# ScalarE's routing one-hots spread over the P·V groups by a table, and the third batch's placing steps moved ahead of its choice of expert

## The chip, the cores and the metric

One core of one Trainium2 chip. The metric is the device time of one execution in microseconds, the median of several; lower is better.

## The reference, cut to what matters

Three layers, one after another. Attention with queries pooled in twos (4 batches, 8 heads, 1152 keys, 576 pooled queries, width 64):

```python
q_pool = q.reshape(B, H, S // 2, 2, D).mean(axis=3)
attn = softmax(q_pool @ k.T / sqrt(D));  x = attn @ v      # x: 2304 tokens of 512
```

Then a mixture of 8 experts in which each token goes to one expert, and a soft mixture behind it:

```python
logits = x @ w_gate + modality_bias[modality_id]
e_idx = np.argmax(logits, axis=1)                          # the routing
out[mask] = gate_w[mask, None] * (np.maximum(x[mask] @ w1[e], 0) @ w2[e])
```

The change is in how the routing of the tokens is worked out while attention is still running. No arithmetic of it changes.

## The kernel before, in words

Attention goes over 16 **pairs** of heads, `p` = 0 to 15, four to a batch: batch 0 is pairs 0 to 3, and so on. A pair has 36 **positions** (`pos`): 2 halves of the queries, 9 blocks of 128 keys, 2 heads. Each position is two matmuls on TensorE, `S1` (L252) and `S2` (L258), into one of three PSUM banks named `sc`, and one exp on ScalarE (`e<-sc`, L262). So an exp that comes late holds up the `S1` three positions on. `maxpiece` (L203, L205) is a matmul into one of three banks `mx` and a maximum on VectorE; it looks for the row maxima of the next pair, and `maxrow` (L223, L226) writes them into `QL`, without which the next pair can't start.

Every sixth position (2, 8, 14, 20, 26, 32) ends with a **group**: the P·V matmuls of three key blocks (`pv`, L272), during which TensorE makes no scores and ScalarE has room, and three additions `acc` on GpSimd (L283, L285), which sum the exps for the softmax. An `e` tile (9 buffers) comes free when its P·V and its addition are done. Besides the exps, ScalarE has in fixed places: at 2 and 8 the casts of a later pair (`KC` twice, `QC`, L158 and L168), at 14 and 26 the copy `sgS` (L310), at 2 and 20 the copy `xu` (L275).

All engines take their instructions in the order in which the program was written; there is no planner. The routing of a batch is written as a list of small steps, `queue`, put together by `in_order` at position 18 (`RT`) of pairs 4, 8 and 12, and at certain positions one step is taken from it:

- `choose`: six VectorE steps that find each token's expert; `gates`: an exp on ScalarE, four VectorE steps (L415 to L418) and the DMA that stores the tokens (`xs`); `rest`: steps that do nothing.
- `place`: `ranks` (TensorE, L357 to L361), five small VectorE steps that end with the conversion `rdf` (L398), then **one-hots**: 24 activations on ScalarE (`far`, L373, and `rA` or `rR`, L374, alternating, two for each of 12 matrices), then `table` (TensorE, L367), which multiplies them.
- `count`: two VectorE steps (L410, L411) that keep the running counts per expert.

One-hots are not taken one by one: at each of the six group positions up to `NHOT` = 4 of them are issued ahead of the group. For batch 0 the four choosing steps and the gates fall in pair 4, ranks and placing in pair 5, one-hots at 26 and 32 of pair 5 and at 2, 8, 14 and 20 of pair 6, the table at 22 of pair 6, the counts behind it; batch 1 likewise in pairs 8 to 10.

For batch 2 (pairs 12 to 14) there is a further list: `expert` (L976 to L991) picks the expert with the most rows, so that its weights can be fetched early by two GpSimd DMAs (`ahead.fetch(0)`, `fetch(1)`, L744), and `rows` comes behind the table. There the order before is ranks, counts, three rests, expert, the two fetches, the five placing steps, one-hots, table. The one-hots fall in pair 14, whose group positions also hold a cast on ScalarE (`split`, L765, 128x512) and a subtraction on VectorE (L766) of the fetched weights.

Of the kernel before, what the change touches and what calls it, by code (L numbers as in the profile page):

```python
# [17 lines left out]
HP = H // 2  # L18
# [19 lines left out]
HPOS = 4  # L38
NI = N // 128
NB = E * (N // TS)  # L40
NHOT = 4
XW = DM + 8
QSTEP = 2
GS = 3
LAG = 3
# [11 lines left out]
MR = (29, 32)  # L57
# [4 lines left out]
RT = 18  # L62
# [24 lines left out]
def attention(ctx, tc, g):  # L87
# [27 lines left out]
    ahead = g["ahead"] = Ahead(tc, g, KS, KH, QS, QL, KX, QX, KC, KL, QLc, QC, VT)  # L115
    pairs = [(b, hp) for b in range(B) for hp in range(HP)]
    n = len(pairs)
# [18 lines left out]
    def load_v(p):  # L136
        b, hp = pairs[p]
        nc.sync.dma_start(out=st[p]["v"], in_=vT[b, hp])
# [51 lines left out]
    def maxpiece(p, m):  # L190
        s = st[p]
        j, blk, t = pieces[m]
        ks = slice(t * 384, (t + 1) * 384)
        mps = ps.tile([128, 512], F32, name="mps", tag="mx", bufs=3)
        if j is None:
            if p == 0:
                for j in range(2):
                    nc.tensor.matmul(mps[:, :384], s["QB"][:, j], s["KS"][:, j, ks], start=(j == 0), stop=(j == 1))
            else:
                nc.tensor.matmul(mps[:, :384], QB, KC[:, ks], start=True, stop=True)  # L200
            slot = 8
        else:
            nc.tensor.matmul(mps[:, :384], s["QS"][:, j, blk * 128:(blk + 1) * 128], s["KS"][:, j, ks], start=True, stop=True)  # L203
            slot = 4 * j + blk
        V.reduce_max(s["mxp"][:, slot, t:t + 1], mps[:, :384], axis=AX.X)  # L205
# [81 lines left out]
    def group(p, g_):  # L287
        steps = range(GS * g_, GS * g_ + GS)
        for step in steps:
            PV(p, step)  # L290
        for step in steps:
            if (p, step) != (n - 1, 2 * NKB - 1):
                accadd(p, step)
# [129 lines left out]
    def in_order(r, select=None):  # L423
        choose, place, count, gates = r

        rest = [lambda: None] * 3
        if select is None:
            return choose[:4] + rest[:2] + gates + choose[4:] + rest[:1] + place + count
        expert, rows = select
        place = place[:1] + count + rest + expert + [lambda i=i: ahead.fetch(i) for i in range(2)] + place[1:]  # L430
        return choose[:3] + rest + gates + choose[3:] + rest + place + rows[:1] + rest + rows[1:]

    def first():

# [100 lines left out]
    nc.sync.dma_start(out=wgbd[0:64, :, 0:E], in_=wg[0])  # L535
    nc.sync.dma_start(out=wgbd[64:128, :, E:2 * E], in_=wg[1])
    consts = g["route_consts"]()
    queue = []
    for p in range(n + 1):
        work = {}  # L540

        def at(pos, *fs):
            work[pos] = work.get(pos, []) + list(fs)

        mp = lambda q, m: (lambda: maxpiece(q, m))
        NP = len(pieces)
        if p == 0:
            for i, m in enumerate(range(NP0, NP)):
                at(P0[0] + i * P0[1] // 8, mp(0, m))
            at(P0[0] + P0[1] + 1, lambda: maxred(0, [3, 4]))  # L550
            at(P0[0] + P0[1] + 2, lambda: maxrow0(0, [(288, 384), (384, 512), (512, 576)]))
            for i, m in enumerate([24, 25, 26] + list(range(24))):
                at(P1[0] + i * P1[1] // NP, mp(1, m))
            for i in range(3):
                at(33 + i, mp(2, 24 + i))
        elif p + 1 < n:
            for pos, m in zip(MA1, range(24)) if p == 1 else zip(MA, range(3, 24)):
                at(pos, mp(p + 1, m))
            if p + 2 < n:
                for pos, m in zip(MB, (24, 25, 26, 0, 1, 2)):  # L560
                    at(pos, mp(p + 2, m))
        if p + 2 < n:
            for pos, f in zip(PREP0 if p == 0 else PREP, prep(p + 2, nc.gpsimd if p == 0 or p >= HP and p % HP < 2 else None)):
                at(pos, f)
        if p < n:
            if p + 1 < n:
                late = 3 if p == 0 else 0
                at(MR[0] + late, lambda: maxred(p + 1, [0, 1, 2, 3, 4]))
                at(MR[1] + late, lambda: maxrow(p + 1))
            late = 4 if p in (0, n - 1) else 2 if p >= HP and p % HP == 0 else 0  # L570
            at(FA[0] + late, lambda: fin0(p, 0))
            at(FA[1] + late, lambda: fin1(p, 0))
            if pairs[p][1]:
                at(FA[2], lambda: fin2(p, 0))
        if p > 0:
            if pairs[p - 1][1] == 0:
                at(FC, lambda: fin2(p - 1, 0))
            fb = FE if p < 4 else FB if p < n - HP else FZ
            at(fb[0], lambda: fin0(p - 1, 1))
            at(fb[1], lambda: fin1(p - 1, 1))  # L580
            if p < n:
                at(fb[2], lambda: fin2(p - 1, 1))
                if pairs[p - 1][1] == HP - 1:
                    at(RT, lambda: queue.extend(in_order(route(pairs[p - 1][0]), ahead.select() if p == n - HP else None)))
        if p == n - 2:
            for i in range(2, 6):
                at(AF2[i - 2], lambda i=i: ahead.fetch(i))
            for i in range(6):
                at(6 * i + 2, lambda i=i: ahead.split(i))
        if p == n - 1:  # L590
            at(0, lambda: ahead.fetch(6), lambda: ahead.fetch(7))
            at(14, lambda: ahead.load_x(0), lambda: ahead.load_x(1))
            at(26, lambda: ahead.turn(0))
            at(28, lambda: ahead.turn(1))
            at(29, ahead.gates)
            for i in range(6):
                at(6 * i + 2, lambda i=i: ahead.split(6 + i))
        if p == n:
            group(n - 1, 2 * NKB // GS - 1)
            assert not queue  # L600
            mm, ev = ahead.mm, ahead.ev

            def both(*fs):
                return [f[i] for i in range(max(map(len, fs))) for f in fs if i < len(f)]

            mm(0)
            ev(0)
            fin0(n - 1, 1)
            mm(1)
            fin1(n - 1, 1)  # L610
            ev(1)
            choose, place, count, gates = route(B - 1)
            ta, tb = g["make_tasks"](ps, count)
            rest = gates[1:]
            run = lambda fs: [f() for f in fs]
            run(choose[:3])
            mm(2)
            run(both(choose[3:], gates[:1]))
            fin2(n - 1, 1)
            ev(2)  # L620
            mm(3)
            place[0]()
            ta[0]()
            ev(3)
            mm(4)
            mm(5)
            table = place.pop()
            chain = both(place[1:], ta[1:], rest)
            for i, f in enumerate(chain):
                f()  # L630
                if i in TAIL:
                    u = 4 + TAIL.index(i)
                    ev(u)
                    if u < 6:
                        mm(u + 2)
            mm(8)
            mm(9)
            table()
            mm(10)
            tb[0]()  # L640
            cut = lambda u: (lambda: ahead.split(u))
            g["rest"] = [cut(12), cut(13), lambda: mm(11), cut(14), cut(15)] + [lambda u=u: mm(u) for u in range(12, 16)] + [lambda: ev(15)]
            break

        units = [(u, c, j) for u in range(2) for c in range(NKB) for j in range(2)]
        for z in units[:3]:
            S1(p, *z)
        for pos, z in enumerate(units):
            if pos >= 3:
                S1(p, *z)  # L650
            S2(p, *z)
            for f in work.get(pos, []):
                f()
            if p and pos % CST == 0 and consts:
                consts.pop(0)()
            if queue and pos >= (8 if p < n - 3 else 0) and (pos % 3 < 2 if p % HP == 0 or p > n - HP else pos % QSTEP == 0) and callable(queue[0]):
                queue.pop(0)()
            if pos % (2 * GS) == LAG - 1:
                for _ in range(NHOT):
                    if queue and not callable(queue[0]):  # L660
                        queue.pop(0)[1]()
            if pos == LAG - 1 and p > 0:
                group(p - 1, 2 * NKB // GS - 1)
            elif pos >= 2 * GS and pos % (2 * GS) == LAG - 1:
                group(p, pos // (2 * GS) - 1)
            if pos == 3 and p + 3 < n:
                if p == 0:
                    load_v(2)
                load(p + 3)
# [1071 lines left out]
```

## Time and profile before

| what | value |
|---|---|
| median of 3 runs | 814.7 us (814.34 to 814.75) |
| the profiled execution | 816.65 us, of which the span from first to last instruction is 814.9 us |
| TensorE busy | 782.9 us, 96% of the span |
| VectorE / ScalarE / GpSimd busy | 565.8 / 461.2 / 541.8 us |
| granted TensorE clock | 0.996 |

Busy shares are means over the whole program. Whether an engine with time to spare still holds up TensorE is read from a stretch of it, here from one pair of heads and from single positions in it.

### The profile page before, as it was taken

The page shows a single profiled execution, that of the slowest core. Times are in us where ns is not written, and L with a number is a line of the kernel's source. Part 1 is how long each engine was busy: PE and PEld are TensorE (multiplying, and loading weights), DVE is VectorE, ACT ScalarE, POOL GpSimd, SP SyncE. Part 2 cuts the span into 40 slices and gives each one's busy share as a digit, 9 for nine tenths or more (in the row PEclk, how much of TensorE's full clock was granted, in tenths as well). Part 3 has the DMA queues.
Part 4 walks back from the last instruction along what each step waited for, and adds up shares of the span by engine and source line. Part 5 has one row for each costly group of instructions (what it writes and reads, how often), then busy time and mean ns, then how long its engine had stood idle before and what let it go on. Part 6 is the DMA issues. An engine that isn't in the chain of part 4 may idle for free.

```text
span 814.9 us, 15864 instructions
## 1 busy us (share of the span) xinstructions
PE 782.9 (96%) x5674; PEld 595.9 (73%) x5674; DVE 565.8 (69%) x1171; ACT 461.2 (57%) x1096; POOL 541.8 (66%) x501
## 2 busy tenths in 40 slices
PE   5899999999999999999999999999999999999897
PEld 5677777766677776777666668788898689988356
DVE  7587777678777877877878785766666556664252
ACT  5456565666865658766556873455555545554133
POOL 6879899999888988879978963534635544450200
PEclk9999999999999999999999999999999999999999
DMA  9876558667655676755554120786787887767987
GB/s 323 232 208 157 156 146 221 158 172 178 148 158 149 149 199 168 176 136 151 127 141 140 52 80 12 223 291 237 274 279 264 261 287 260 272 208 260 341 364 233
DMA packets 57782, 162.80 MB, mean 200 GB/s; under 512 B 14443, under 2 KB 21915, under 8 KB 53595
## 3 DMA queue, kind: packets, MB, share of 16 engines
q1 hardware_dynamic: 41604, 98.05, 42.7%
q0 software_dynamic: 13648, 47.32, 17.4%
q10 hardware_dynamic: 2448, 16.39, 5.6%
q8 instruction: 46, 0.75, 0.4%
q14 instruction: 36, 0.29, 0.1%
HBM read 110.45 MB, written 10.89 MB: 149 GB/s over the span
## 4 chain that ended last, share of the span: by engine, by line
PE 82%; DVE 5%; ACT 4%; POOL 3%; issue 3%; DMA 2%; SPq 0%; ACTq 0%; POOLq 0%; DVEq 0%
PE pv L272 17%; PE sc L252 12%; PE sc L258 8%; PE mps L203 7%; PE hp L774 4%; PE hp L776 4%; PE hp L775 4%; PE yp L788 4%; PE yp L790 3%; PE yp L789 3%; PE sg L305 2%; PE hp L1472 2%; PE op L1486 2%; PE tp L332 2%; DVE mxp L205 1%
## 5 line engine op out<-in xcount | busy, mean ns | idle before, releaser
L285 POOL TENSOR_TENSOR acc<-acc,e 128x576 f32<-128x576 f32 x214 | 315.2, 1473 | 23.6 <-ACT e L262 10.1
L262 ACT ACTIVATE e<-sc 128x288 f32<-128x288 f32 x576 | 223.7, 410 | 138.8 <-PE sc L258 116.1
L205 DVE TENSOR_REDUCE mxp<-mps 128x1 f32<-128x384 f32 x432 | 220.5, 549 | 94.2 <-PE mps L203 86.4
L252 PE MATMUL sc<-QS,KS 128*128 128x288 f32 x576 | 186.0, 331 | 3.3 <-ACT e L262 3.1
L258 PE MATMUL sc<-QL,KH 69*128 69x288 f32 x576 | 170.0, 298 | 1.5 <-DVE QL L223 1.2
L272 PE MATMUL pv<-e,V 128*64 128x288 f32 x1152 | 161.8, 416 | 0.0
L252 PEld LDWEIGHTS sc<-QS,KS 128*128 128x128 f32 x576 | 109.2, 190 | 56.4 <-issue 27.1
L203 PE MATMUL mps<-KS,QS 128*128 128x384 f32 x384 | 134.9, 356 | 11.5 <-ACT QS L468 7.0
L744 POOL DMA_INDIRECT wraw<-in_w,widx x72 | 73.9, 1026 | 106.3 <-DVE wlo L766 82.7
L272 PEld LDWEIGHTS pv<-e,V 128*64 128x64 f32 x1152 | 74.4, 137 | 60.2 <-issue 22.2
L258 PEld LDWEIGHTS sc<-QL,KH 69*128 69x128 f32 x576 | 109.3, 190 | 2.0 <-DVE QL L223 1.4
L766 DVE TENSOR_TENSOR wlo<-wraw,whi 128x512 fp32r<-128x512 f32 x136 | 90.7, 689 | 27.1 <-ACT whi L765 22.8
L765 ACT CAST whi<-wraw 128x512 fp32r<-128x512 f32 x136 | 79.6, 619 | 18.2 <-DMA wraw<-in_w,widx 14.0
L203 PEld LDWEIGHTS mps<-KS,QS 128*128 128x128 f32 x384 | 74.4, 194 | 14.8 <-ACT QS L468 7.4
L774 PE MATMUL hp<-xh,whi 128*128 128x256 f32 x256 | 73.2, 286 | 0.0
L776 PE MATMUL hp<-xh,wlo 128*128 128x256 f32 x256 | 71.9, 281 | 1.0 <-issue 0.8
L775 PE MATMUL hp<-xl,whi 128*128 128x256 f32 x256 | 71.8, 280 | 0.3 <-DVE xl L761 0.3
L283 POOL TENSOR_TENSOR acc<-e 128x576 f32<-128x576 f32 x31 | 44.7, 1441 | 35.8 <-ACT e L262 35.7
L781 ACT ACTIVATE hh<-hp 128x256 fp32r<-128x256 f32 x64 | 24.5, 384 | 72.8 <-PE hp L776 55.6
L782 DVE SCALAR_TENSOR_TENSOR hl<-hp,hh 128x256 fp32r<-128x256 f32 x64 | 27.1, 424 | 42.7 <-ACT hh L781 39.6
L788 PE MATMUL yp<-whi,hh 128*128 128x512 f32 x128 | 53.0, 414 | 0.7 <-ACT hh L781 0.6
L774 PEld LDWEIGHTS hp<-xh,whi 128*128 128x128 f32 x256 | 48.1, 188 | 4.8 <-ACT whi L765 1.3
(397 smaller groups left out, 1233.2 us busy)
## 6 DMA issues: line engine op xcount, KB each, us to landing
mw<-in_m2w SPq DMA_DIRECT2D x17, 1024.0 KB, 6.8
mw<-in_m2w ACTq DMA_DIRECT2D x15, 1024.0 KB, 7.2
V<-in_vT SPq DMA_DIRECT2D x16, 576.0 KB, 3.6
KX<-in_kT SPq DMA_DIRECT2D x15, 576.0 KB, 4.0
QX<-in_qT SPq DMA_DIRECT2D x15, 576.0 KB, 5.9
KS<-KC SPq DMA_DIRECT2D x30, 288.0 KB, 5.3
KH<-KC SPq DMA_DIRECT2D x30, 288.0 KB, 4.6
QS<-QC SPq DMA_DIRECT2D x60, 144.0 KB, 3.9
```

The source lines that it names most:

```text
L203: nc.tensor.matmul(mps[:, :384], s["QS"][:, j, blk * 128:(blk + 1) * 128], s["KS"][:, j, ks], start=True, stop=True)
L205: V.reduce_max(s["mxp"][:, slot, t:t + 1], mps[:, :384], axis=AX.X)
L252: nc.tensor.matmul(sc[:, :NU], s["KS"][:, j, c * 128:(c + 1) * 128], s["QS"][:, j, u * NU:(u + 1) * NU], start=True, stop=False)
L258: nc.tensor.matmul(sc[:, :NU], s["KH"][0:69, j, c * 128:(c + 1) * 128], s["QL"][0:69, j, u * NU:(u + 1) * NU], start=False, stop=True)
L262: nc.scalar.activation(s["e", u, c][:, j], sc[:, :NU], AF.Exp, scale=SM)
L272: nc.tensor.matmul(pv[j * 64:(j + 1) * 64, :NU], s["v"][:, j, c, :], e[:, j], start=(c == 0), stop=(c == NKB - 1))
L285: eng.tensor_add(s["acc", u], s["acc", u], s["e", u, c])
L766: nc.vector.tensor_sub(lo, x, hi.bitcast(F32))
L774: nc.tensor.matmul(hp, wh[:, c], xh[:, k], start=(k == 0), stop=False)
L775: nc.tensor.matmul(hp, wh[:, c], xl[:, k], start=False, stop=False)
L776: nc.tensor.matmul(hp, wl[:, c], xh[:, k], start=False, stop=(k == DM // 128 - 1))
L788: nc.tensor.matmul(yp[h], hh[:, hs], wh, start=(f == 0), stop=False)
```

## The change

- `NHOT` becomes a table by position (2, 0, 2, 2, 2, 4 at 2, 8, 14, 20, 26, 32), and `NHOT2` (3, 3, 3, 3, 3, 4) for pair 14. So 24 one-hots spread over more groups: for batch 0 from 26 of pair 5 to 20 of pair 7, for batch 2 from 26 of pair 13 to 32 of pair 14.
- The one-hots get a list of their own, `hots`, which is drawn on once the step `ready` has run; the queue goes on meanwhile, so `count` now runs in pair 5 (at 28 and 30). When the list is empty, what must follow (`after`: the table, for batch 2 also `rows`) is put in the queue.
- In pairs 4 and 8 one step is taken at every position below 29, where before it was at two positions of three up to the end; one rest less stands ahead of the gates.
- Batch 2: the placing steps stand among the expert steps, ahead of the fetches. Taken one by one, the expert steps stood at 18, 19, 21, 22, 24, 25 of pair 13 and the fetches at 27 and 28; now they stand at 18, 21, 25, 27, 28, 30 and at 31 and 33. Placing, which stood at 30 to 34 and at 0 of pair 14, is at 13, 15, 16, 19 and 22.

```diff
-NHOT = 4
+NHOT = {2: 2, 8: 0, 14: 2, 20: 2, 26: 2, 32: 4}
+NHOT2 = {2: 3, 8: 3, 14: 3, 20: 3, 26: 3, 32: 4}
...
+        hots.extend(f[1] for f in place if not callable(f))
+        table = [place.pop()]
+        place = [f for f in place if callable(f)]
+        ready = lambda: hot.append(True)
         if select is None:
-            return choose[:4] + rest[:2] + gates + choose[4:] + rest[:1] + place + count
+            return choose[:4] + rest[:1] + gates + choose[4:] + rest[:1] + place + [ready] + count, table
         expert, rows = select
-        place = place[:1] + count + rest + expert + [lambda i=i: ahead.fetch(i) for i in range(2)] + place[1:]
-        return choose[:3] + rest + gates + choose[3:] + rest + place + rows[:1] + rest + rows[1:]
+        place = (place[:1] + count + place[1:4] + expert[:1] + place[4:5] + expert[1:2] + place[5:] + [ready] + expert[2:]
+                 + [lambda i=i: ahead.fetch(i) for i in range(2)])
+        return choose[:3] + rest + gates + choose[3:] + rest + place, table + rows[:1] + rest + rows[1:]
...
-            if queue and pos >= (8 if p < n - 3 else 0) and (pos % 3 < 2 if p % HP == 0 or p > n - HP else pos % QSTEP == 0) and callable(queue[0]):
+            if queue and pos >= (8 if p < n - 3 else 0) and (pos % 3 < 2 if p >= n - HP else pos < MR[0] if p % HP == 0 else pos % QSTEP == 0):
                 queue.pop(0)()
-            if pos % (2 * GS) == LAG - 1:
-                for _ in range(NHOT):
-                    if queue and not callable(queue[0]):
-                        queue.pop(0)[1]()
+            if pos % (2 * GS) == LAG - 1 and hot:
+                for f in hots[:(NHOT2 if p == n - 2 else NHOT)[pos]]:
+                    hots.pop(0)()
+                if not hots:
+                    hot.clear()
+                    queue.extend(after)
+                    after.clear()
```

## Rows read from the trace of the kernel before

**Rows 1.** Exps in stretches of one pair: stretch, length, busy (count), clock, DMA, GB/s

```profile
170.60:201.65 31.05, 14.05 (x36) 1.00 0.87 221
201.65:232.20 30.55, 13.78 (x36) 1.00 0.56 147
232.20:260.60 28.40, 14.20 (x36) 1.00 0.60 159
...
288.95:318.87 29.92, 13.95 (x36) 1.00 0.90 229
...
406.25:438.45 32.20, 14.21 (x36) 1.00 0.59 155
438.45:469.30 30.85, 13.02 (x36) 1.00 0.22 69
```

**Rows 2.** ScalarE in order of time, position 8 of pair 6

```profile
207.39 0.66 ACT L158 CAST KC<-KX 128x576 fp32r<-128x576 f32 x1
...
208.53 0.36 ACT L373 ACTIVATE far<-i,rdf 96x72 f32<-96x72 f32 x1
...
209.27 0.49 ACT L373 ACTIVATE far<-i,rdf 96x256 f32<-96x256 f32 x1
...
210.21 2.37 ACT L262 ACTIVATE e<-sc 128x288 f32<-128x288 f32 x6
```

**Rows 3.** ScalarE in order of time, position 8 of pair 7 (in brackets: idle before)

```profile
239.16 2.51 ACT L262 ACTIVATE e<-sc 128x288 f32<-128x288 f32 x6 [0.47 <-PE sc L258]
```

**Rows 4.** TensorE in order of time, ranks in pair 5

```profile
181.21 0.26 PE L357 MATMUL rp<-oh,trir 96*96 96x48 f32 x1
...
182.10 0.46 PE L272 MATMUL pv<-e,V 128*64 128x288 f32 x2
```

**Rows 5.** TensorE in order of time, table in pair 6

```profile
220.33 0.87 PE L367 MATMUL tbp<-rR,rA 96*72 96x256 f32 x6
221.04 0.29 PE L252 MATMUL sc<-QS,KS 128*128 128x288 f32 x1
```

**Rows 6.** VectorE in order of time, second half of pair 4

```profile
163.18 0.56 DVE L205 TENSOR_REDUCE mxp<-mps 128x1 f32<-128x384 f32 x1 [1.16 <-PE mps L203]
...
166.32 1.04 DVE L416 TENSOR_SCALAR sm<-sm 96x6 f32<-96x6 f32 x1
...
170.07 0.75 DVE L418 COPY xr<-sm 96x48 f32<-96x48 f32 x1
```

**Rows 7.** TensorE in order of time, first positions of pair 5

```profile
171.34 0.45 PE L203 MATMUL mps<-KS,QS 128*128 128x384 f32 x1 [0.48 <-DVE mxp L205]
```

**Rows 8.** ScalarE in order of time, position 2 of pair 14

```profile
439.50 0.61 ACT L765 CAST KS<-KX 128x512 fp32r<-128x512 f32 x1
440.62 0.35 ACT L373 ACTIVATE far<-i,rdf 96x72 f32<-96x72 f32 x1 [0.50 <-DVE rdf L398]
```

**Rows 9.** VectorE in order of time, expert steps of batch 2 in pair 13

```profile
426.90 1.28 DVE L988 TENSOR_SCALAR aone<-akey,amx 128x8 f32<-128x8 f32 x1
...
430.59 0.15 DVE L991 SCALAR_TENSOR_TENSOR awidx<-aex,pioq 128x4 int32<-128x4 f32 x1
```

**Rows 10.** GpSimd in order of time, around the first fetches

```profile
428.24 1.41 POOL L285 TENSOR_TENSOR acc<-acc,e 128x576 f32<-128x576 f32 x1
431.05 1.24 POOL L744 DMA_INDIRECT KX<-in_w,awidx  x1 [1.40 <-DVE awidx L991]
...
438.14 0.97 POOL L744 DMA_INDIRECT KX<-in_w,awidx  x1
439.12 5.29 POOL L285 TENSOR_TENSOR acc<-acc,e 128x576 f32<-128x576 f32 x3
```

**Rows 11.** GpSimd in order of time, last additions of pair 14

```profile
471.24 4.75 POOL L285 TENSOR_TENSOR acc<-acc,e 128x576 f32<-128x576 f32 x3
```

**Rows 12.** ScalarE in order of time, positions 15 and 16 of pair 15

```profile
479.44 0.74 ACT L262 ACTIVATE e<-sc 128x288 f32<-128x288 f32 x2 [1.10 <-PE sc L258]
```

**Rows 13.** A stretch behind the third fetch: all engines' busy time, clock, DMA share, GB/s

```profile
439.70:441.90 2.20, 2.20 (x19) 1.57 (x15) 2.20 (x4) 1.63 (x5) 2.12 (x2) 1.00 0.81 238
```

More of the change, by code (lines that the diff above doesn't have):

```diff
@@ L537, in attention, with begin @@
     consts = g["route_consts"]()
-    queue = []
+    queue, hots, hot, after = [], [], [], []
+    def begin(now, later):
+        queue.extend(now)
+        after.extend(later)
     for p in range(n + 1):
@@ L583, in attention @@
                 if pairs[p - 1][1] == HP - 1:
-                    at(RT, lambda: queue.extend(in_order(route(pairs[p - 1][0]), ahead.select() if p == n - HP else None)))
+                    at(RT, lambda: begin(*in_order(route(pairs[p - 1][0]), ahead.select() if p == n - HP else None)))
         if p == n - 2:
@@ L599, in attention @@
             group(n - 1, 2 * NKB // GS - 1)
-            assert not queue
+            assert not queue and not hots and not after
             mm, ev = ahead.mm, ahead.ev
```

## The prediction

> **What bounds the kernel now.** I read the profile's first page, then the exps of ScalarE pair by pair, then single positions in the order of time, then the list of waits. TensorE is busy 96% of the span at full clock, so only time that TensorE loses can be won. Since the engines take their work in program order, the pairs of attention are copies of one another, and a longer pair shows what disturbed it. An undisturbed pair takes 28.40 us (pair 7; pairs 4, 8 and 12 are within 0.1 of it). The pairs with routing behind them take 31.05, 30.55 and 29.92 (pairs 5, 6 and 9; pair 10 repeats pair 6), and batch 2's take 32.20 and 30.85 (pairs 13 and 14) [rows 1]. The excess is 4.80 for batch 0, some 3.65 for batch 1 (1.52 and the repeated 2.15) and 6.25 for batch 2: 14.7 us in all. The question is how much of it the new places free.
>
> The reader is to see how the one-hots lengthen a pair. At position 8 of pair 6 ScalarE runs two casts from 207.39 and four one-hots from 208.53, with no idle time, and the next exp starts only at 210.21 [rows 2]. At the same place of pair 7, without one-hots, ScalarE has 0.47 us left over before its next exp [rows 3]. So the four take 1.68 where 0.47 is free. The delay of the exp is 1.2 or so, of which TensorE, with two more score banks in hand, gets back a few tenths. The one-hots come in twos: 0.74 us for the pair on 72 columns (208.53 to 209.27) and 0.94 on 256 (209.27 to 210.21) [rows 2].
>
> **What must stay.** Ranks hold TensorE from 181.21 to 182.10, 0.89 us [rows 4], and the table from 220.33 to 221.04, 0.71 us [rows 5]. Both are only moved (the table from pair 6 to pair 7). A pair that opens a batch also ends with fewer transposes and passes them on to the next one; I put 0.3 on that, an estimate, about a third of the 0.89 that the eight matmuls of ranks take. That is 1.9 us per batch that no placing can remove.
>
> **Batches 0 and 1.** The excess of batch 0 less 1.9 is 2.9; that of batch 1 is 1.75.
>
> - The one-hots at 2 and 8 of pair 6 are 2.15 less the table's 0.71, so 1.45 us of it, in batch 1 the same. Position 8 gets none now. Position 2 gets one pair of 0.94 instead of 1.68, in front of the `xu` copy that waits for P·V anyway. I take both as gone. The groups at 14, 20 and 26 get 0.74 to 0.94; less than half of what they hid or nearly hid before. Position 32 keeps four, which before cost nothing there. Bounds: all of it gone, or 0.3 left at two positions of each batch.
> - What is left, 1.45 in batch 0 and 0.3 in batch 1, is the late start of pair 5 and the first one-hots at 26, where four waited for `rdf` and two will now. The start: at the end of pair 4 VectorE is late, as the gates' L416 (1.04) and L418 (0.75) fall among the row maxima [rows 6], and TensorE waits for a maximum 0.48 us before it can load position 1's piece [rows 7]. One step per position brings these gates to 25 to 27, and there VectorE sat idle for 1.16 us [rows 6]. I take that stall as gone. If the front-loaded steps are late there, 0.5 comes back in each of pairs 4 and 8.
> - Cost: `count` moves into the end of pair 5 (and 9) ahead of `maxrow`. Its addition is of the kind of L416, 1.04 us [rows 6], or nothing if VectorE has that idle time; from the stall of 0.48 [rows 7] at the upper end to 0, I take 0.15 per batch. Late next would be `QL` for the next pair.
>
> Sum: 2.9 - 0.15 = 2.75 and 1.75 - 0.15 = 1.6, together 4.35 us, between 3.0 and 4.65.
>
> **Batch 2, pair 14.** Before, the first four one-hots waited 0.50 us for `rdf` behind the cast [rows 8], then took their 1.68. With `rdf` in pair 13, and three in place of four at five of the six groups, 0.4 us leaves each of them. Pair 14's excess is 2.45, of it the table 0.71; of the other 1.7 I take 1.4 as gone. ScalarE's room at such a group is about 1.6 to 2.0: the 2.82 from the first cast to the exp at position 8 of pair 6 less the 1.2 by which it was too much, and the few tenths that the banks hide [rows 2]. The cast's 0.61 and three one-hots (1.3) are 1.9, just inside it. Bounds 0.8 and 1.7.
>
> **Batch 2, pair 13.** The placing steps that came at its end now stand among the expert steps; `ranks`, the store of `xs` and the counts stay where they were. In the trace L988 takes 1.28 and L991 0.15, both on 128x4 or 128x8 [rows 9]; L416, on 96x6, took 1.04 [rows 6]. So a small VectorE step costs 0.15 to 1.3 us here, and five moved ones add 0.75 to 6.5 to the stretch from 13 to 22, with L395 to L398 likely about half that. They delay row maxima and may hold TensorE; L988 and L989, which sat before `sgS` at 26, move past it. I take these to cancel but for a gain of 0.5, bounds -1.0 and +0.8.
>
> **Batch 2, GpSimd.** This is what I looked for a new wait in. `fetch(0)` waited for `awidx`, written at 430.59, and began at 431.05 [rows 9, 10]. The step that writes it goes from position 25 to 30. Those five positions hold the group at 26: at 28.40 us for 36 positions five are 4 us, and VectorE's lag may shrink or grow, so I take `awidx` at 435.0, bounds 434.0 and 437. GpSimd works in program order, and the three additions of the group at 32 stand behind `fetch(0)`, `fetch(1)` behind them. From 435.0: 1.24 for the fetch [rows 10], three additions of 1.41 to 1.48 [rows 10], then two fetches of 0.97, which ends near 442.7 where the trace had the next additions begin at 439.12 [rows 10]. That is 3.6 late, or about 3.4, since these additions took 5.29 rather than 4.4 [rows 10], some of which will not recur. GpSimd has little idle time after it, so pair 14's last addition, which ended at 475.99 (471.24 + 4.75) [rows 11], ends near 479.4. The exp at position 16 of pair 15 needs the buffer that this frees. It began at about 479.8, as the second from 479.44 [rows 12], so 3.8 us of slack. With 3.4 of it gone and TensorE 1.9 earlier, ScalarE would wait 1.5 us. TensorE hides part of it with its score banks, and I take 0.75 as lost, bounds 0 and 2.5.
>
> The weights themselves: a tile of 0.5 MB that was issued at 438.14 [rows 10] has its bytes moved by 441.9 (238 GB/s for 2.20 us is that tile) [rows 13], 3.8 us. From 435.0 it lands at 438.8; the first cast began at 439.50 with no idle time before it [rows 8] and will come 0.5 earlier. It is just in time. If `awidx` is at its upper bound, ScalarE stands 2 us at position 2.
>
> Sum for batch 2: 1.4 + 0.5 - 0.75 = 1.15, between -2.5 and 2.5.
>
> In all 4.35 + 1.15 = 5.5 us. The profiled execution took 816.65 with a span of 814.9, so I expect a span near 809.4 and 811.15 with what lies around it; that execution is 1.95 above the median of the runs, and on the median of 814.7 the forecast is 809.2. A saving in attention should reach the end whole, since what follows waits for the routing of the last batch.
>
> **The rivals.**
>
> - *GpSimd takes all of batch 2's gain, and more.* If `awidx` comes at 437, the late additions and the late weights together cost about 2.5 more than I took. For it: the slack of 3.8 [rows 12] is nearly used. Against: it needs VectorE to lag 2 us more than I take, on top of the 4.4 by which `awidx` moves. Total gain 2.0 to 2.5 (2.0 for the additions, about 1 for the cast at position 2), time near 812.5.
> - *The moved steps are blocked, and the time gets worse.* Suppose that each of the five moved steps takes 1.3 as L988 did [rows 9]. Then `awidx` is 6.5 us later still, at 441, the additions are 9.9 late against 3.8 of slack [rows 12], and from a lag of about 9 us on batch 2 loses more than the 4.35 won elsewhere: about 9.9 - 3.8 = 6.1 lost, time 816.4. Against it: L991 among the same neighbours took 0.15, so not every step is hit. Of the trace's two kinds of duration the Trainium skill gives a reason (SBUF — State Buffer, Who interferes with whom): VectorE and GpSimd share a port pair that one instruction holds from start to end, and a VectorE step with two SBUF inputs or in a two-port mode is shut out for as long as the GpSimd one lasts. By that rule a moved step costs up to one addition (1.41), the five up to 7 us, and the time would be 817; the 1.28 of L988 agrees, the 0.15 of L991 is a case in which nothing was in the way.
> - *The bursts were not what cost.* If the excess of pairs 6 and 10 were TensorE's own work, spreading would move and not free it; only the stall at the start of pair 5 and the wait for `rdf` go, 1 to 1.5 us, time 813.5. Against it: ScalarE is gapless at position 8 of pair 6 and idle in pair 7 [rows 2, 3].
>
> **How the numbers follow.** The forecast with its bounds (gain 3.5 to 7) has 0.65, a gain above 7 has 0.05, GpSimd taking batch 2's gain 0.16, bursts not the cause 0.07, worse 0.07. The measurement of this kernel can tell 0.2%, 1.6 us, from no change. Of the third rival about half lies within 1.6, and a little of the first: faster 0.86, same 0.07, slower 0.07. The range: below, a gain of 7.0, nearly all upper bounds together (4.65 + 2.5), 807.7, and I go to 807.4; above, the first rival at 812.5 and a little beyond, 812.8. That leaves out the third rival, the worse one, and the few best cases.
>
> **What would show it.** Pair 6 and pair 10 near 28.4, pairs 7 and 11 near 29.1 (the table), pairs 5 and 9 near 29.7, pair 14 near 29.4 and pair 13 near 31.7. ScalarE idle again before the exp behind position 8 of pair 6. At the start of pair 5 no wait of TensorE for a maximum. `awidx` near 435 and the last additions of pair 14 some 2 to 3 us nearer to the exp that needs them, with waits of exps on GpSimd in pair 15. The forecast is wrong if pairs 7 and 11 grow by more than the table, if pair 5 keeps its late start or pair 9 gets one from the counts, or if pair 15 stretches by more than 1 us.

## The result and the profile after

The change makes the kernel slower: 821.03 us against 814.73 (medians of 6 runs each), ratio 1.007 with a 95% interval of 1.0042 to 1.0097 (ratios here compare all executions, so they can differ from the quotient of two medians). The forecast was 809.2, range 807.4 to 812.8. The six executions spread from 817.56 to 823.78 and the mean granted clock goes along, from 0.994 in the fastest to 0.987 in the slowest; the kernel before stayed within 814.2 to 816.4. The profiled execution is the fastest of them (817.56, span 815.8), so its rows show the least of the loss.

Pair by pair, as in [rows 1], with pairs 8 and 10 besides:

```profile
169.10:199.65 30.55, 14.09 (x36) 1.00 0.63 175
199.65:228.05 28.40, 14.20 (x36) 1.00 0.61 158
228.05:257.15 29.10, 14.22 (x36) 1.00 0.60 155
257.15:287.05 29.90, 14.23 (x36) 1.00 0.62 152
287.05:317.30 30.25, 14.26 (x36) 1.00 0.66 186
317.30:345.75 28.45, 14.20 (x36) 1.00 0.60 158
...
403.25:436.90 33.65, 14.20 (x36) 1.00 0.51 132
436.90:471.95 35.05, 13.71 (x36) 0.90 0.23 75
```

Pairs 6 and 10 are down from 30.55 to 28.4, an undisturbed pair, and pair 7 is up by the table's 0.7: the one-hots are hidden, as forecast. Pair 5 went from 31.05 to 30.55 only, pair 9 from 29.92 up to 30.25, and pair 8, undisturbed before, to 29.90. From pair 4 to 12 the sum fell by 1.7 us (264.15 to 262.45). Then batch 2 gives it back and more: pair 13 from 32.20 to 33.65, pair 14 from 30.85 to 35.05, with a mean clock of 0.90 in it.

The spans of the two profiles differ by only 0.9, since two stretches outside these pairs were shorter after the change. Pair 4 starts at 140.80 instead of 142.10: the profile before has its clock at half for a while in pair 0, which the change does not touch, and the profile after does not. TensorE's busy time there, with the clock behind the count:

```profile
33.90:37.30 3.40, 3.40 (x16) 0.50 1.00 376
```

Behind pair 14 it is another 1.75, which was not followed up.

**Pair 14.** TensorE in the order of time around position 26, the idle time before an instruction in brackets, and GpSimd's last additions before it:

```profile
456.01 0.29 PE L259 MATMUL sc<-QL,KH 69*128 69x288 f32 x1
459.78 0.69 PE L306 MATMUL sg<-acc,ones 128*32 128x288 f32 x2 [3.48 <-POOL acc L286]
```

```profile
456.86 2.87 POOL L286 TENSOR_TENSOR acc<-acc,e 128x576 f32<-128x576 f32 x2
```

`sg` sums the exps of the first half of the queries from `acc`. The addition that it needs ends at 459.73, and TensorE, which takes its work in order, stands still for 3.48 us. In the kernel before the same addition ended at 458.41 and `sg` began at 459.27, 0.86 us to spare. Counted from the start of pair 14 the addition is 2.87 later than before (22.83 instead of 19.96) and TensorE is there 1.42 earlier (19.40 instead of 20.82): these two, less the 0.86 to spare, make 3.43 of the 3.48. So 1.4 of the wait is time that TensorE had won by the new places of batch 2's steps and one-hots.

```profile
456.66 1.75 POOL L285 TENSOR_TENSOR acc<-acc,e 128x576 f32<-128x576 f32 x1
```

```profile
459.27 0.44 PE L305 MATMUL sg<-acc,ones 128*32 128x288 f32 x2
```

Why GpSimd is late is in its own order of time, which answers to [rows 10]:

```profile
427.28 1.41 POOL L286 TENSOR_TENSOR acc<-acc,e 128x576 f32<-128x576 f32 x1
432.87 1.24 POOL L758 DMA_INDIRECT KX<-in_w,awidx  x1 [4.18 <-ACT e L263]
434.15 4.43 POOL L286 TENSOR_TENSOR acc<-acc,e 128x576 f32<-128x576 f32 x3
438.73 1.31 POOL L758 DMA_INDIRECT QX<-in_w,awidx  x1 [0.15 <-issue]
```

GpSimd sits idle for 4.18 us ahead of the fetch, where it was 1.40. The index `awidx` is written at 432.41, and the additions of the group at 32, the first of which had its exps by then, stand behind the fetch in program order. (The bracket names an exp; the fetch itself reads only the index.)

During the stall the clock falls. Busy time of all engines by stretch, with the granted clock behind the counts:

```profile
450.00:458.00 8.00, 6.19 (x43) 4.78 (x42) 5.42 (x13) 5.49 (x15) 7.61 (x6) 1.00 0.01 2
458.00:464.80 6.80, 5.02 (x21) 2.27 (x22) 2.11 (x1) 2.08 (x5) 6.18 (x6) 0.50 0.39 128
464.80:472.00 7.20, 7.04 (x50) 5.42 (x48) 5.40 (x13) 5.17 (x14) 6.51 (x6) 1.00 0.09 27
```

6.8 us at 1.2 GHz, of which the first 1.8 belong to the stall itself.

**Pair 13.** Two of the moved placing steps on VectorE, and the transposes on TensorE that wait behind them:

```profile
418.49 0.90 DVE L396 CAST rdi<-dest 96x6 int32<-96x6 f32 x1
419.31 0.54 DVE L206 TENSOR_REDUCE mxp<-mps 128x1 f32<-128x384 f32 x1
419.77 1.10 DVE L397 TENSOR_SCALAR rdi<-rdi 96x6 int32<-96x6 int32 x1
```

```profile
420.00 0.38 PE L318 MATMUL sgT<-ident,sgS 80*96 80x80 f32 x3 [0.93 <-DVE mxp L206]
...
421.39 0.53 PE L333 MATMUL tp<-ident,xu 128*96 128x128 f32 x3 [0.53 <-DVE mxp L206]
```

The steps work on 96x6 numbers and take 0.90 and 1.10. They stand between row maxima; these free the PSUM banks that `sgT` and `tp` share with them. The two waits make 1.46 us. In the kernel before, TensorE waited in pair 13 elsewhere, in front of `sg`, and this wait is gone:

```profile
428.79 0.44 PE L305 MATMUL sg<-acc,ones 128*32 128x288 f32 x2 [0.53 <-DVE mxp L205]
```

So the growth of 1.45 is a net figure: some 2.0 paid, of which 0.5 shows in no single wait, and 0.53 won. Experiment 7 separates the two.

**Pair 8.** The same kind of thing in the front-loaded choosing steps:

```profile
274.65 1.42 DVE L388 TENSOR_TENSOR lg<-lg,sm 96x48 f32<-96x48 f32 x1
275.99 0.54 DVE L206 TENSOR_REDUCE mxp<-mps 128x1 f32<-128x384 f32 x1
276.45 1.09 DVE L389 SCALAR_TENSOR_TENSOR rtmp<-lg,wt 96x48 f32<-96x48 f32 x1
```

```profile
276.58 0.44 PE L204 MATMUL mps<-KS,QS 128*128 128x384 f32 x1 [1.13 <-DVE mxp L206]
```

TensorE waits 1.13 us there for a maximum. It did not in pair 4, with the same list at the same positions: there L388 and L389 took 0.19 each.

### The profile page after: what moved, and what is told of

Same layout as the page of the kernel before. It is cut to its first block, busy times and chain, and to the rows that moved or that the text cites. A ratio compares the mean times of both kernels' runs of the same rounds, so it can differ in the third digit from the quotient of the medians.

```text
span 815.8 us, 15858 instructions
## 1 busy us (share of the span) xinstructions
PE 783.0 (96%) x5674; PEld 596.0 (73%) x5674; DVE 561.2 (69%) x1171; ACT 464.0 (57%) x1096; POOL 544.6 (67%) x501
## 4 chain that ended last, share of the span: by engine, by line
PE 86%; DVE 7%; DMA 3%; issue 2%; POOL 1%; ACT 1%; SPq 0%; POOLq 0%; ACTq 0%; DVEq 0%
PE pv L273 18%; PE sc L253 12%; PE sc L259 9%; PE mps L204 8%; PE hp L788 4%; PE hp L790 4%; PE hp L789 4%; PE yp L802 4%; PE yp L804 4%; PE yp L803 4%; DVE mxp L206 2%; PE sg L306 2%; PE hp L1486 2%; PE op L1500 2%; PE tp L333 1%
## 5 line engine op out<-in xcount | busy, mean ns | idle before, releaser
L796 DVE SCALAR_TENSOR_TENSOR hl<-hp,hh 128x256 fp32r<-128x256 f32 x64 | 27.1, 424 | 40.5 <-ACT hh L795 39.3
```

## The experiments

Theory G: in batch 2 the late fetch idles GpSimd, its additions come late, and `sg` waits. Rivals: V, the front-loaded VectorE steps; H, the one-hots and placing steps of pairs 13 and 14. In the cuts of the edits `...` stands for parts left out and `fetches` for the two fetches. Times are medians; each ratio is to the kernel before on the same chip (814.0 to 814.5).

| kernel | us | ratio, 95% interval | pair 13, 14 in its profile |
|---|---|---|---|
| changed kernel | 821.03 | 1.007 (1.0042 to 1.0097) | 33.65, 35.05 |
| 1 batch 2 as before | 812.34 | 0.998 (0.9964 to 0.9996) | 32.18, 30.83 |
| 2 fetch behind additions | 817.3 | 1.0024 (0.9999 to 1.0049) | 37.80, 29.46 |
| 3 sg later | 817.3 | 1.0033 (1.0006 to 1.006) | 36.81, 29.87 |
| 4 batch 2's part alone | 820.47 | 1.0078 (1.0062 to 1.0094) | 36.64, 34.21 |
| 5 old pace in pairs 4, 8 | 812.66 | 0.999 (0.9982 to 0.9999) | 32.17, 30.85 |
| 6 old pace in pair 8 | 811.26 | 0.9969 (0.9956 to 0.9981) | 32.19, 30.85 |
| 7 three idle steps | 815.43 | 1.0024 (1.001 to 1.0039) | 34.25, 30.85 |
| 8 placing, then fetch | 811.51 | 0.9973 (0.9959 to 0.9986) | 32.78, 29.98 |
| 9 counts behind the table | 811.1 | 0.9956 (0.9942 to 0.9971) | 32.19, 30.83 |
| 10 filled wait | 821.75 | 1.0084 (1.0066 to 1.0102) | 36.19, 33.72 |

**1. Batch 2 as before.**

```diff
-        place = (place[:1] + count + place[1:4] + expert[:1] + ... + [ready] + expert[2:] + fetches)
+        place = place[:1] + count + rest + expert + fetches + place[1:] + [ready]
-NHOT2 = {2: 3, 8: 3, 14: 3, 20: 3, 26: 3, 32: 4}
+NHOT2 = {2: 4, 8: 4, 14: 4, 20: 4, 26: 4, 32: 4}
```

> Batch 2 in the order of the kernel before (expert and both fetches ahead of placing, four one-hots at every group of pair 14), the rest of the change kept. Theory G (in batch 2 the fetch stands so late in GpSimd's program order that the additions behind it come late, and the sg matmul at position 26 of pair 14 waits for them, after which the clock falls): no such wait, clock 0.996, time 812 to 813.5, 1.2 to 2.7 below the kernel before. Rival V (the front-loaded choosing steps of pairs 4 and 8 cost what is lost): stays at 816 or above.

812.34: pairs 13 and 14 are again as in the kernel before, and the rest of the change is worth 0.2%. The loss is in batch 2, not in pairs 4 and 8.

**2. The fetches behind the additions.**

```diff
-... + [ready] + expert[2:] + [fetch(0), fetch(1)]
+... + [ready] + expert[2:] + rest[:1] + [fetch(0), fetch(1)]
```

> The changed kernel with one empty step ahead of the two fetches, so that they stand at 33 and 34 of pair 13, behind the three additions of the group at 32 in GpSimd's order. Theory G: GpSimd does these additions while it waits for the index (432.6 in the changed kernel), the fetch begins within 0.5 us of where it did, the wait at position 26 of pair 14 and the fall of the clock go, time 810.5 to 813. Rival H (the one-hots and the placing steps in pairs 13 and 14 are what costs): unchanged at 817 to 823, since neither moves.

Pair 14 goes from 35.05 to 29.46: one empty step, which puts the first fetch too behind the three additions of the group at 32 (the second stood there already), removes the wait and its fall of the clock. The one-hots stayed where they were, so in pair 14 they are not what costs. GpSimd is no longer held up ahead of the fetch (0.60 us):

```profile
435.89 2.91 POOL L286 TENSOR_TENSOR acc<-acc,e 128x576 f32<-128x576 f32 x2 [0.69 <-ACT e L263]
439.39 1.24 POOL L758 DMA_INDIRECT KX<-in_w,awidx  x1 [0.60 <-ACT e L263]
```

Yet the median is 817.3, outside what G expected, since pair 13 took 37.80. Its clock fell at 424.0, right behind the two waits for VectorE, for 6.8 us:

```profile
414.00:424.00 10.00, 8.42 (x58) 5.92 (x58) 9.01 (x16) 4.36 (x11) 8.66 (x6) 1.00 0.81 181
424.00:430.80 6.80, 6.80 (x27) 4.38 (x26) 2.65 (x8) 1.63 (x4) 0.58 (x1) 0.50 0.36 83
```

This profile has a second fall that is not of the change's making, 6.8 us at half clock from 31.5 in pair 0, and pair 13 has one more wait, of 0.86. The fastest of its six executions took 811.57 at a mean clock of 0.998, four others 816.9 to 818.4 at 0.990 to 0.992. So G alone does not explain the result: a second loss sits in pair 13 (theory M), in the moved steps, part of H.

**3. sg later.**

```diff
-            late = 4 if p in (0, n - 1) else ...
+            late = 4 if p in (0, n - 2, n - 1) else ...
```

> The changed kernel with sg of pair 14 at position 30 instead of 26 (its two followers later too). Theory G puts the loss at this one wait: four positions with a group between are about 4 us, so the wait of 3.5 us falls below 0.7, the clock stays up, time 812 to 815. If GpSimd is late for more than this one reader, the wait turns up at the exps (for an e tile) in pairs 14 and 15, and the time stays at 816 to 820.

The wait shrinks from 3.48 to 0.73 and pair 14 takes 29.87: the loss in pair 14 was at this one reader. GpSimd is still late; a second wait of 1.07 for `acc` turns up at the next `sg`, in pair 15, not at an exp. The time is 817.3; in the profile (821.81, the slowest of the six) pair 13 had its fall of the clock (36.81), and the clock fell at 33.0 and 56.9 too.

**4. Batch 2's part alone.**

```diff
-            return choose[:4] + rest[:1] + gates + choose[4:] + rest[:1] + place + [ready] + count, table
+            return choose[:4] + rest[:2] + gates + choose[4:] + rest[:1] + place + [ready], table + count
-(pos % 3 < 2 if p >= n - HP else pos < MR[0] if p % HP == 0 else ...)
+(pos % 3 < 2 if p >= n - HP or p % HP == 0 else ...)
-hots[:(NHOT2 if p == n - 2 else NHOT)[pos]]
+hots[:(NHOT2 if p == n - 2 else NHOT)[pos] if p > n - HP else 4]
```

> The kernel before with the batch 2 part alone: new order in pair 13, one-hots of batch 2 by the two tables; batches 0 and 1 with four one-hots per group and the old steps. Theory G: all of the loss and none of the gain, the changed kernel plus the 1.7 us won in pairs 4 to 12: 819 to 825, granted clock 0.985 to 0.994. Rival V: no slower than the kernel before, 813 to 815.

820.47, the whole loss, with the 3.48 us wait in pair 14 and clock falls in pairs 13 (6.8 us) and 14 (3.4 us).

**5 and 6. The old pace.** On the kernel of experiment 1:

```diff
-(pos % 3 < 2 if p >= n - HP else pos < MR[0] if p % HP == 0 else ...)
+(pos % 3 < 2 if p >= n - HP or p % HP == 0 else ...)      # 5: pairs 4 and 8
+(pos % 3 < 2 if p >= n - HP or p == 2 * HP else ...)      # 6: pair 8 alone
```

> The kernel of the first experiment (batch 2 as before) with the old pace in pairs 4 and 8 too (two positions of three, up to the end), so that of the change only the spread one-hots and the earlier counts of batches 0 and 1 are left. If the front-loaded steps are what made pair 8 longer (29.94 against 28.35), pair 8 goes back to 28.4 and pair 5's late start of 0.7 returns: net 0.9 better than the first experiment, 811 to 812. If pair 8 is longer for another reason it stays at 29.9.

> As the one above, but with the old pace in pair 8 alone. Front-loading pays in pair 4 and costs in pair 8: both are then at their better value, 810.5 to 811.5, some 1.6 below the first experiment. If it is a matter of chance which VectorE steps are held behind a GpSimd addition, pair 4 or pair 8 comes out longer again by 0.5 to 1.5.

In both, pair 8 falls from 29.9 to 29.0 (not to the 28.4 expected; with one rest less its steps still stand one place earlier than in the kernel before, and what is left was not followed up beyond a wait of 0.35 for a maximum at 281.11 in 6). In 5 pair 5 is 31.8, in 6 it is 30.5: front-loading helps pair 4's successor and harms pair 8. Kernel 6 is 1.1 below experiment 1, which ran on another chip, and 1.4 below 5, which ran on the same one.

**7. Three idle steps.** On the kernel of experiment 1, in place of the three rests at 13, 15 and 16 of pair 13:

```diff
+        spare = [
+            lambda: V.tensor_reduce(sd, tmp, op=ALU.add, axis=AX.X),
+            lambda: V.tensor_copy(si[:, :, 0], sd),
+            lambda: V.tensor_single_scalar(si[:, :, 1], si[:, :, 0], 8, op=ALU.logical_shift_right),
+        ]
-        place = place[:1] + count + rest + expert + ...
+        place = place[:1] + count + spare + expert + ...
```

> The kernel of the first experiment with three more small VectorE steps on tiles that nobody reads, of the kinds of L394 to L396, where three empty steps stand in pairs' routing of batch 2 (13, 15 and 16 of pair 13). Theory M (the moved placing steps themselves hold VectorE there, TensorE waits for row maxima and the clock falls): pair 13 goes from 32.2 to 33.5 or, where the clock falls, to 36 to 38; time 1.3 to 5 above the first experiment. Rival F (pair 13 is longer because of what follows the fetch): pair 13 stays at 32.2.

Three steps that nobody reads make pair 13 34.25 long instead of 32.18, and the waits are those of the changed kernel to the hundredth:

```profile
420.65 0.38 PE L318 MATMUL sgT<-ident,sgS 80*96 80x80 f32 x3 [0.93 <-DVE mxp L206]
...
422.04 0.53 PE L333 MATMUL tp<-ident,xu 128*96 128x128 f32 x3 [0.53 <-DVE mxp L206]
...
428.49 0.44 PE L306 MATMUL sg<-acc,ones 128*32 128x288 f32 x2 [0.53 <-DVE mxp L206]
```

The last row is the wait in front of `sg` that the changed kernel had got rid of: here it stays, and pair 13 is 0.6 longer than there.

Its eleven executions go from 813.3 at a clock of 0.999 to 818.6 at 0.991; the profiled one has no fall in pair 13. So the place of the steps, not what they compute, costs 2 us: this part of M is shown. That the two waits also bring the fall of the clock is argued: of the six profiles with these waits four have it right behind the second of them (2, 3, 4) or the first (10), and of the six without none has a fall in pair 13.

**8. Placing, then fetch.** On kernel 6:

```diff
-count + rest + expert + fetches + place[1:] + [ready]
+count + rest + expert + place[1:] + fetches + [ready]
```

> As the second of this call, with batch 2's placing steps behind the expert steps (27 to 33 of pair 13) and the two fetches behind those (34 of pair 13 and 0 of pair 14), so behind the additions of the group at 32 in GpSimd's order, and the conversion done before the first one-hots. By theory G the index is as early as before and GpSimd waits for nothing, pair 14 starts without the 0.5 wait: 810 to 811. If the first weights come too late for the cast at 2 of pair 14, ScalarE waits there and pair 14 is longer than 30.8.

Pair 14 falls to 29.98, pair 13 rises to 32.78; together 0.28 better than in 6, which the times (811.51 and 811.26) don't show.

**9. Counts behind the table.** On kernel 6:

```diff
-... + place + [ready] + count, table
+... + place + [ready], table + count
```

> The kernel of old pace in pair 8 (batch 2 as before, pair 4 front-loaded, one-hots of batches 0 and 1 spread) with the counts of batches 0 and 1 behind the table again, so in pairs 7 and 11. If the 1.06 us addition ahead of maxrow is what holds the end of pair 9, pair 9 comes out 0.5 shorter (30.5 to 30.0) and pair 5 the same or a little shorter, time 0.3 to 1.0 below that kernel, 810.2 to 811. If pair 9 stays, it is chance of where GpSimd's additions fall.

Pair 9 falls from 30.51 to 29.90 and pair 5 from 30.53 to 29.70; pair 4, whose program is that of kernel 6, took 29.37 against 28.32 in this execution, with a wait of 0.71 for a maximum that kernel 6 did not have there. 811.1, ratio 0.9956: the best ratio of all, though its interval overlaps those of 6 and 8, and faster than the kernel before and the changed one.

**10. The wait filled.** On the changed kernel, ahead of `sg` of pair 14:

```diff
+        for _ in range(15):
+            nc.tensor.matmul(o[:, 0:128], ident, ident, start=True, stop=True)
```

> The changed kernel with 15 extra 128-column matmuls on the identity, which wait for nothing, ahead of sg of pair 14, where TensorE otherwise stands still for 3.5 us for GpSimd's addition. The sums are still late, so the wait stays about as long in all. If the stillness is what drops the clock there, the granted clock stays at 1.0 behind it and pair 14 takes about 1.5 to 3 less than 35.0, the time 1.5 to 3 below the changed kernel's 821. If the clock falls there for another reason, pair 14 stays at 34 to 35 with 6.8 us of half clock, and the extra work only adds.

In the profile the clock stays up behind the filled wait (1.00 where it had been 0.50) and pair 14 is 1.3 shorter (each of the 15 is recorded as two):

```profile
460.37 3.51 PE L553 MATMUL busy<-ident 128*128 128x128 f32 x30
464.03 0.44 PE L306 MATMUL sg<-acc,ones 128*32 128x288 f32 x2
```

```profile
460.30:463.90 3.60, 3.58 (x32) 3.39 (x30) 0.56 (x1) 0.74 (x3) 3.44 (x3) 1.00 0.00 0
463.90:470.00 6.10, 5.12 (x38) 3.26 (x38) 3.71 (x7) 4.99 (x13) 5.47 (x6) 1.00 0.59 172
```

The median did not follow (821.75). The profiled execution, the slowest of the six, had its fall in pair 13 again, one of 3.4 us in pair 0 and another of 6.8 at 767, far behind attention. Whether keeping TensorE busy at one place only moves the fall to others is open.

## Why the prediction was wrong

- **What bounds it, what must stay, the one-hots: right.** Pairs 6 and 10 lost 2.15, the table's 0.7 came back in pairs 7 and 11. Pair 14 without the wait (experiment 2) is 29.46, down 1.4, as forecast.
- **Batches 0 and 1: sign right, size too big.** 4.35 was forecast, at least 3.0, and 1.7 came. The lower bound was too high for its own terms: 4.65 less 1.2 for the one-hots, 0.96 for the counts and 1.0 for the front-loaded steps is 1.5. The late start of pair 5 went, but pair 5 got a wait of 0.53 for VectorE at 189.31, among placing steps of over a microsecond (L397 1.40, L398 1.24). Front-loading cost 1.55 in pair 8, of which the lower bound had 0.5. The counts cost pair 9 some 0.6 (experiment 9), not 0.15: the addition took 1.06 right ahead of `maxrow`, and TensorE waited 0.25 for `QL` at 315.54, the reader that the prediction named.
- **Batch 2, pair 13: wrong sign.** I took the moved steps to cancel with a gain of 0.5, bounds -1.0 and +0.8. They cost about 2.0 at full clock, and experiment 7 shows the three that fall at 13 to 16 to be enough; the gain of 0.5 did come (the wait in front of `sg`), so the pair lost 1.45. Their price was in the prediction (0.15 to 1.3 each); what I left out is what is queued behind them: the transposes of `sgT` and `tp` at 17 and 18, which need the same banks as the maxima.
- **Batch 2, GpSimd: the step that failed.** The mechanism was the one I looked for, and its size was nearly right: `awidx` came 4.8 us later within the pair (29.2 after the start of pair 13 instead of 24.3; I had 4.4), the additions of pair 14 that `sg` needs 2.9 (I had 3.4). But I followed the late additions only to the e tile at position 16 of pair 15, with 3.8 to spare [rows 12]. The first reader on TensorE is `sg` at position 26 of pair 14, with 0.86 to spare and not 3.8. The wait there is 3.48 where I had 0.75, an exp's wait less what the banks hide; here TensorE itself waits, and nothing hides it. With the clock behind it pair 14 grew by 4.2, where I had it 1.4 shorter.
- **The clock: not priced at all.** I treated time lost by TensorE as lost once. The 3.48 us stall came with 6.8 us at half clock, and with 3.4 in experiment 4; with the stall gone (2, 3) or filled (10) there was no fall in pair 14. Behind the two waits of pair 13 the clock fell in profiles 2, 3, 4 and 10 and not in those of the changed kernel and of 7. Pair 13 takes 36.2 to 36.8 with the fall (3, 4 and 10; the 37.8 of 2 has one more wait of 0.86) and 33.65 without, 2.5 to 3.2 us. That would fit most of the distance from the changed kernel's profile to its median. But the clock also fell in pair 0, which is the same in all these kernels, in the profiles of the kernel before, 2, 3, 9 and 10. Of the executions without a profile only the mean clock is known, so where theirs fell, and how much of the spread of 6.2 us is the change's, is argued and not shown.
- **The rivals.** The nearest was GpSimd taking all of batch 2's gain; at 812.5 it was priced too low for both reasons above. The one on the slower side, with 0.07, named the blocked steps in pair 13 but asked for a delay of the index that did not come: the five steps took 0.16 to 1.10, not 1.3 each. By the port rule of the Trainium skill (SBUF — State Buffer, Who interferes with whom) four of them could each have cost, by estimate, up to one addition, 1.41; the fifth, L395, is a reduction, which that section excepts on trn2, so the prediction counted one too many (L395 took 0.18). The trace has both kinds: L397 took 1.10 and ended when a GpSimd addition did (420.87 and 420.86), L398, of the same form on the same tile, took 0.16 at 423.44, when GpSimd was idle (from 422.21 to 425.77).

## What to carry to other kernels

When a transfer that waits for an index is moved, list what stands behind it on its own engine, and follow the late work to its first reader on the bound engine, not to the reader with a buffer. If that transfer can stand behind the work that is ready, one place in the order is enough (experiment 2). A small vector step that is held for a microsecond holds up what is queued behind it, on its own engine and on TensorE, so its place among the maxima matters more than its 0.2 us; and where the bound is TensorE, count a stall with the half-clock time that may follow it.

## What the runs showed of the hardware that was not expected

The granted clock fell to 0.50 for 6.8 us after waits of 0.93 and 0.52 us within three microseconds (experiment 2, at 424.0), and did not after the same two waits in another profile (experiment 7, clock 1.00). And the same steps of pair 4 took 28.32 us in one execution and 29.37 in another (experiments 6 and 9), the second of which had its clock at 0.50 from 32.5 to 39.3, in pair 0: L389 took 0.19 in the one and 1.49 in the other. That a small shift between VectorE and GpSimd decides which small steps are held fits this, but was not tested.
